# A transformer block on one core: the written-out order of all engines and the PSUM banks replaced, waits sorted, unused constants removed

## The chip, the core and the metric

One NeuronCore of a Trainium2 chip runs the whole program in one launch. Five engines have a queue of their own and run it in order: PE (matmuls), ACT (activations), DVE (elementwise work and PSUM readout), POOL (a few small operations) and SP (issues every DMA). They meet only in semaphores. The metric is the device time of one execution in microseconds. Three runs of the kernel before gave 1084.05, 1085.04 and 1085.25 us; the median is 1085.04.

## The reference: what is computed

Input `x` has 2048 rows of 1024, in bfloat16. With LN a layer norm without weights:

```
q = (LN(x) @ wq) in 32 heads of 32;  k = LN(x) @ wk;  v = LN(x) @ wv     # k, v: one head, shared
h = x + (softmax(q k^T / sqrt(32)) v, heads joined) @ wo
g = LN(h) @ w_gate;  u = LN(h) @ w_up                                   # 1024 -> 3584
out = h + (sigmoid(g) * u) @ w_down                                     # 3584 -> 1024
```

## The kernel before

**Tiles.** The rows are cut into 16 tiles of 128. Attention works on half tiles: one of 32 `hf` values takes 128 queries and 16 of the 32 heads, so 4 groups of 32 partitions by 512 columns. One *visit* (`emit_S`, L858) takes one `hf` and one of 16 blocks of 128 keys: four score matmuls that run side by side on 32 rows of the array each (row mode) fill four of six score banks of PSUM (`S_ps`), and two exponentials on ACT, 128x1024 each, write probabilities into a slot of `Pr`. There are 512 visits and 1024 exponentials. `mk_PV` multiplies probabilities by values (four matmuls side by side on 32 columns each, column mode), DVE adds the probabilities up (`make_add`, L850), `mk_SUM` sums them over the keys, and `finish` divides. `mk_OP` applies `wo` for a tile, and DVE adds `x`, takes the statistics and normalises.

**Feed-forward.** For each tile 14 groups `mk_GU` follow (7 slices of 512 columns, each a gate group *g* and an up group *u*; 8 matmuls of 512 columns): ACT takes tanh of *g* into one buffer `tnh` (L1246), DVE forms (tanh+1)*u into `act_s` (L1267), and a DMA transposes it into `hact`. Two groups `mk_D` of 28 matmuls each apply `w_down`. Gate and up weights stream from HBM through a ring and, at the end, through the free slots of `Pr` (`load_next`, 256 KB per DMA).

**Array modes.** Scores run in row mode. Between two visits a matmul of 128 columns of weights runs whole (dense) unless a column-mode group lies between the same two visits; then it is issued as four quarter matmuls (`choose_modes`, L152), so that the array changes its mode only twice a visit.

**Two working banks.** All groups but the scores (PV, SUM, OP, Q, KV, GU, D, the transposes; 472 of them) accumulate in the two banks of `F_ps`. A group is numbered when the planner begins it (`begin`, L1337), and its bank is the digit of `BANKS` under that number. The first matmul of a group waits until the group before it in the same bank has been read out by ACT or DVE.

**The order.** A planner (`Plan`) runs the program on estimated costs and gives one list of operations per engine. `reorder` (L113) then permutes each list by a string in `ORDER`: pairs of characters, of which the first says how far the next piece lies beyond the lowest operation not yet taken, and the second how many operations in a row are taken. All five engines run exactly that order. The lists hold 5757 operations on PE, 1152 on ACT, 1090 on DVE, 60 on POOL and 1017 DMAs on SP.

**The waits.** `emit` (L1518) keeps the largest value to wait for on each semaphore and issues the waits in the order in which the dependencies stand:

```
for d in o.deps + [d for d in o.order if d.eng != e]:
    ...
    if d.val > want.get(k, (0, None))[0]:
        want[k] = (d.val, s)
for k, (val, s) in want.items():
    if waited.get(k, 0) < val:
        eng.wait_ge(s, val)
```

**Constants.** `TUNE["bc"]` is 0, so `ONCHIP` is empty and `mk_BC` is never called; `pickt` (POOL, three operations) and `third` (DVE, three operations) are computed and never read.

Of the kernel before, what the change touches and what calls it, by code (L numbers as in the profile page):

```python
# [8 lines left out]
F32 = mybir.dt.float32  # L9
ACTF = mybir.ActivationFunctionType  # L10
ALU = mybir.AluOpType
# [16 lines left out]
        '0~0B32030=21020A12010~0i32030e72070iq4g20g08120105210201q392090f120102q892090f210209q3j20j01a204030252050242'  # L28
        '040252050242040252050242040252050242040252050242043272529103014202410201520501a22702014204034204033202680103'
        '013203034204033203034204033203034203560102034204024204033701a2020102420403420403320302y1f20f0h01320303225802'  # L30
        '014802abndX1l2Yc0201220203s6A142B404015203v8o202010e210202a631624282ihg2030821020o26020s26020gq832030f320301'
        '0u28020h28020362060o2202j2y4D20j0dk2010h027201a305j201020b7207c604e8u2m8w508t20t0g210208a762060202a205220201'
        '0b41125101010512010e12010V12010382320303011201a4024204021201a202a24204021201a204220202041b010311010513011201'
        '05120108120106124801010d220201110101613203010d22020722020321012401a35205030122020461220202051301622202020431'
        '0302120104622202020k12010g1201061242010102120101a203320182019101022202a2033203020122020512010528c1a202051201'
        '0512010522020542040422020j110171013203010212010612010812010512012502011201a104320301031501015132610301a23203'
        '052202230222014801010224015201320304220207220204320151015201012202a201b152c1050201220204320304220135a282c101'
        '0322020361420403220132010233030322020722020432030181083203054204034201720182c1026202044204034202510222015203'
        '110102427104015205226242810182e20102420151926101022101210101420242015182010203b20b0332030472529303b202510201'
        '01320234a27201010332030542026a0201e2010241012272439201420403420402420402513268f2e1h3033203582202010412010532'  # L40
        '03723402710111520103018208720371035101016203215201a2017203a20101040152050452025202a2010501520501c20c52050162'
        '0601820801520264c2a2e2030101625185e20552a273c3i2010263c2920291c2i201010153c2820192d101i2010164d2019101920252'
        '01610163c201810202018208620603620601820837031101320306320303420253020101420403326101610201420334927101012202'
        '01420245b2910191010242130103a202a3f2080204320304520503320302825205013203019102420171030103322154b292d1020152'
        '4172018102a273c1010152025103014202510201520502320303420405420402420402a382d208032202028102220202021201082202'
        '07220221012252017101042202042202a104320161023101032201b1010332030233030385080312010l73520283d1b2e1030528b202'
        '0103a13203034201210102a1420403420102033203033203043203034204327352a203022202024278040124020a81080d2202024103'
        '4222610101a3f14201f103b172040b12010812010d13010382080612010p124501816292010518011201011101021201410401120105'
        '12010615017232030202120105124201010312010f22020812010512010c22020722013101041301042202072201c101a101a15201a2'
        '01b1e101b202010322020241025201210101029252050222020253320303227702a1d203h10203b162c202c101c203020242011253e2'  # L50
        '01060162158101520502520501520344b2820191c101420403520113610152050152050332030532030518010e220208120101110102'
        '12010b410405a30132e101e20201620305a2052202010422114601041601410141030q2501610112c3010332910301011201a1051201'
        '0121010d120102a1031281016103430102320304320304220204320231010322020a51017352a102920203a56206020122a202060312'
        '01061201038232a1030312010512010632030342040542040332030522020542830462a802010242015801c202014404013201620241'
        '920204034204024204a1025205013203044304014204054202a1d10201629301b40405320303320304320305420403320302a482e208'
        '0222020118010655c3a205021282019103420161014104220203a2320303420202924204032202042502032102031801021201052202'
        '02734202810181016101011201052202042801a2010102a1013203042202021242316101042202011352417201110132030632030231'
        '6142030332125601320164c1a2d102a1024211010202b20b028152050132030462060342040242040542040252237501f201017903f5'
        '01j501e203i50102b2e80301k2i201l201k10101c2040102720701625185e20501018207920106016206015232780304340301320304'
        '3203236202010432a4g2e2030581b2920801a262060152010202520512620103054204034204045205024204045295g2e2o301q2l201'  # L60
        'r3030202h30202b103050d82080532030r87080I58i8v503x3020503f501j30105510155019101910203350172020683080283056103'
        '01840571030Z'),
    act=(
        '0a11010411010211010211010211010311010211010~0w12010615010113010b13010711010R11010411010511010911010t11010i11'
        '010g11010k11010711010o11010411010411010b11010711010y13010412010211010711010c12010q12010211010711010311010711'
        '010c11010811010h11010311010611010d11010b11010x11010611010311010l11010r11010q11010a11010611010i11010611010x11'
        '010z11010b12010311010h12010c11010511010511010311010611010s11010i12010j12010311010k11010512010k12010911010311'
        '010311010g'),
    dve=(
        '012251416101680108110121021301311251714161840113615101349171013201713101110101113151210121011241319201025211'  # L70
        '0131011132d16101810141015101f1610101312171115191010141013102215201410231022101032102011101011101051101110104'
        '21020151124131610103110105110111018101b1110141c17101c1910111d10151016101114101110131011101120111010311010115'
        '7361b1a1c10112014102110102110101120101210201310381011201021161310102061g01052111011101011101619101a191029101'
        '11a191b10102011201110101110111010111011501210211310101011131012151010131010101210211010113010131030131011101'
        '11011101011101021101031101190102120103110102110106710421117151410101011101124101012102022102011bd10121010721'
        '0205810411310171320111316101114101012102110121021eg1f10104130101110101a102c10231029101a131020171010232010121'
        '022102021571619181a6011101061101011141215131618101010113010311010321021101210218010411010613010a126132010102'
        '114101110111012102114101021241315c0111010b11010221110103110111010112011201110101113101010315716181a191b1d1c1'
        'e1011101032111010111010181061171310101110101110111011101011101041351416ah1g1i2010321020121012101110113514161'
        '810141310131010111011101011101210211011101021b01053101311101210271011101043111010107110111010111011101033102'  # L80
        '27a191c1b1e2d10105120101110102113121427261a20131011101210131010111310101110106146151719181a1c1b1011201011101'
        '11010211010271b10711410101021101110103110105135141620106210201110103110102124101010d'),
    pool=(
        '04d1h1g102d1c101f301h701n104k201l101le01y90101'),
    sp=(
        '01110111011101077151312161410202211152a2410191b1a1018211k121m1f101i131g2116121n1d1q2o181l1f1w1y171u1B4p1m191'
        'b1A1s141j1I1G1x1k1z1e1H1v101c1l1h1k10121a181c101a16131b181i1d141c1e10102210141612211510101110101120104511101'
        '110121011101814101410141014101012101413121010112011101110101715141910151b10161c1023101510101012101215541d1a1'
        '0181012252013371b1610101310152413171012111318142013151410153011101011101091101110131114121629401016101216251'
        '318101010212428171a16191g1f1h1b2k1j1i1l101j1l1k1a2m1o1n1q1p1r6y1A1G1z1C30181a2g1d141c1j2e1h1l1f1i1n2s3r1B1q1'  # L90
# [72 lines left out]
MARG = {"sl": 700.0, "rb": 1000.0, "rd": 1200.0, "ha": 900.0, "hT": 200.0, "ql": 1200.0, "xr": 1500.0, "o": 1400.0, "qs": 900.0, "wd": 700.0}  # L163


class Plan:
# [1429 lines left out]
```

## Time and profile before

| what | value |
|---|---|
| median of three runs | 1085.04 us (1084.05 to 1085.25) |
| profiled execution: span, from the first to the last instruction | 1083.9 us |
| profiled execution: its own time | the page gives the span alone; the median lies 1.1 us above it |
| PE | 1068.8 us busy (99%), 10588 matmuls |
| ACT | 1002.9 us busy (93%), 1008 exponentials into `Pr` of 1077 ns |
| DVE | 866.3 us busy (80%) |
| POOL | 36.1 us busy (3%) |
| DMA | 234.24 MB, 216 GB/s on average |
| mean granted TensorE clock | 0.998 |

The page gives an engine as busy from the start of an instruction to its end. Matmuls overlap: one of 512 columns is shown with 380 ns, while the next starts 216 ns after it. So 99% busy does not say that PE lost 1% only; what it loses is read from the starts of consecutive matmuls. A number in brackets in a timeline row is the time that the engine stood idle before it, and the engine whose work ended that wait.

### The profile page before, as it was taken

What the parts mean: (1) busy time and instruction counts of PE and PEld (TensorE: products, weight loads), DVE (VectorE), ACT (ScalarE), POOL (GpSimd) and SP (SyncE); (2) the same over time, 40 slices, a digit from 0 to 9 for tenths busy, and PEclk for the clock granted to TensorE, in tenths of its full rate; (3) what the DMA queues carried; (4) which work ended last, traced back from release to release, by engine and by line L of the source; (5) the groups of instructions that cost most, each with busy time, mean ns of one, the idle gap of its engine ahead of it and who ended that gap; (6) DMA issues with size and microseconds to landing.
All of it is one profiled execution on the core that took longest, in us unless ns stands there. A gap on an engine that the chain in (4) does not pass through costs nothing.

```text
span 1083.9 us, 25911 instructions
## 1 busy us (share of the span) xinstructions
PE 1068.8 (99%) x10588; PEld 432.3 (40%) x10588; DVE 866.3 (80%) x1090; ACT 1002.9 (93%) x1153; POOL 36.1 (3%) x64
## 2 busy tenths in 40 slices
PE   7999999999999999999999999999999999999998
PEld 6533465333333333333333333333333333333343
DVE  8989997887888887896888788888788878888721
ACT  5999999999999999999999999999999999999310
POOL 3300000000000000000000000000000000000000
PEclk9999999999999999999999999999999999999999
DMA  8767797799767796957968685967848796696994
GB/s 248 120 199 219 213 289 222 221 228 249 226 180 222 189 259 162 275 167 202 277 167 226 173 254 162 269 190 195 253 124 257 222 252 165 196 266 150 316 315 125
DMA packets 298935, 234.24 MB, mean 216 GB/s; under 512 B 102080, under 2 KB 285376, under 8 KB 298816
## 3 DMA queue, kind: packets, MB, share of 16 engines
q1 hardware_dynamic: 298816, 232.58, 77.2%
q8 instruction: 84, 1.38, 0.6%
q14 instruction: 35, 0.29, 0.1%
HBM read 203.55 MB, written 8.11 MB: 195 GB/s over the span
## 4 chain that ended last, share of the span: by engine, by line
PE 81%; ACT 15%; DVE 2%; issue 1%; SPq 1%; DMA 1%; DVEq 0%
PE F_ps L601 59%; ACT Pr L879 13%; PE S_ps L601 13%; PE F_ps L605 9%; ACT tnh L1246 1%; DMA ring<-in_A_x_dram 1%; SPq L453 1%; DVE acc L850 0%; DVE rb L928 0%; SPq L462 0%; ACT QTb L879 0%; ACT hnT L879 0%; ACT hact L879 0%; ACT hact L421 0%; DVE h_sb L1314 0%
## 5 line engine op out<-in xcount | busy, mean ns | idle before, releaser
L879 ACT ACTIVATE Pr<-S_ps 128x1024 bf16<-128x1024 f32 x1008 | 944.0, 1077 | 2.3 <-PE S_ps L601 2.0
L850 DVE TENSOR_TENSOR acc<-acc,Pr 128x2048 bf16<-128x2048 bf16 x429 | 522.9, 1220 | 28.7 <-ACT Pr L879 10.3
L601 PE MATMUL F_ps<-ring,hnT 128*128 128x512 bf16 x1312 | 334.5, 380 | 0.9 <-DVE h_sb L1314 0.3
L601 PE MATMUL S_ps<-QTb,kT 32*128 32x512 bf16 x2048 | 208.1, 385 | 2.1 <-ACT Pr L879 1.6
L601 PE MATMUL F_ps<-zone,hact 128*128 128x512 bf16 x732 | 202.2, 380 | 0.0
L601 PEld LDWEIGHTS F_ps<-ring,hnT 128*128 128x128 bf16 x1312 | 115.0, 97 | 155.9 <-issue 45.3
L601 PE MATMUL F_ps<-Pr,Vt 128*32 128x512 bf16 x2016 | 138.6, 382 | 2.3 <-ACT tnh L1246 1.0
L1267 DVE SCALAR_TENSOR_TENSOR act_s<-tnh,F_ps 128x512 bf16<-128x512 f32 x105 | 71.9, 685 | 82.3 <-PE F_ps L601 69.9
L601 PEld LDWEIGHTS S_ps<-QTb,kT 32*128 32x128 bf16 x2048 | 53.4, 91 | 209.4 <-ACT Pr L879 129.3
L1246 ACT ACTIVATE tnh<-F_ps 128x512 f32<-128x512 f32 x112 | 71.5, 639 | 48.0 <-PE F_ps L601 48.0
L601 PEld LDWEIGHTS F_ps<-zone,hact 128*128 128x128 bf16 x732 | 65.7, 98 | 86.8 <-issue 22.9
L605 PE MATMUL F_ps<-ring,hnT 128*32 128x512 bf16 x1104 | 76.6, 380 | 0.1
L601 PEld LDWEIGHTS F_ps<-Pr,Vt 128*32 128x32 bf16 x2016 | 47.1, 96 | 58.5 <-issue 14.6
L601 PE MATMUL F_ps<-zone 128*128 128x512 bf16 (+3 forms) x537 | 65.0, 266 | 2.4 <-DVE rstd L523 0.9
L601 PE MATMUL F_ps<-wo_sb,OT 128*128 128x512 bf16 x243 | 62.9, 380 | 0.2 <-ACT tnh L1246 0.2
L1034 DVE TENSOR_TENSOR oun<-F_ps,oun 128x512 f32<-128x512 f32 x64 | 44.0, 688 | 23.8 <-PE F_ps L601 23.4
L520 POOL TENSOR_TENSOR dsb<-zb,cst 128x1 bf16<-128x1 bf16 x18 | 17.7, 983 | 964.3 <-DVE zb L517 901.5
L605 PE MATMUL F_ps<-zone,hact 128*32 128x512 bf16 x656 | 48.1, 381 | 0.0
L601 PEld LDWEIGHTS F_ps<-zone 128*128 128x128 bf16 x537 | 34.9, 97 | 25.0 <-issue 7.9
L850 DVE TENSOR_TENSOR acc<-Pr 128x2048 bf16<-128x2048 bf16 x31 | 37.2, 1201 | 0.9 <-ACT Pr L879 0.8
L1097 DVE TENSOR_TENSOR h_sb<-F_ps,h_sb 128x512 bf16<-128x512 f32 x32 | 22.1, 691 | 19.6 <-PE F_ps L601 18.8
L605 PEld LDWEIGHTS F_ps<-ring,hnT 128*32 128x32 bf16 x1104 | 26.4, 96 | 27.4 <-issue 10.2
(94 smaller groups left out, 456.1 us busy)
## 6 DMA issues: line engine op xcount, KB each, us to landing
ring<-in_B_w_up_dram SPq DMA_DIRECT2D x312, 256.0 KB, 4.4
ring<-in_B_w_gate_dram SPq DMA_DIRECT2D x310, 256.0 KB, 4.3
rb<-r_scratch SPq DMA_DIRECT2D x120, 64.0 KB, 3.4
zone<-in_B_w_down_dram SPq DMA_DIRECT2D x14, 512.0 KB, 5.2
Pr<-in_B_w_gate_dram SPq DMA_DIRECT2D x18, 256.0 KB, 5.3
ring<-in_A_x_dram SPq DMA_DIRECT2D x16, 256.0 KB, 6.7
h_sb<-in_A_x_dram SPq DMA_DIRECT2D x16, 256.0 KB, 4.4
out_dram<-h_sb SPq DMA_DIRECT2D x32, 128.0 KB, 3.9
```

The costliest lines, as they stand in the source:

```text
L453: x_ld[t] = dma(lambda: SP.dma_start(x_sb(t), xf[t * P:(t + 1) * P, :]), f"x{t}", P * D * 2, prio=0)
L520: g = pl.op("pool", lambda: POOL.tensor_tensor(out=dsb[:, ph, tk], in0=zb[:, ph, tk], in1=half[:, 0:k], op=ALU.pow), [f, c0], prio=0, **sl ...
L601: return lambda: PE.matmul(o, lhsT=l, rhs=r, start=start, stop=stop, **kw)
L605: f.quads = [(lambda j=j: PE.matmul(o[DH * j:DH * (j + 1)], lhsT=l[:, DH * j:DH * (j + 1)], rhs=r, start=start, stop=stop, tile_position=( ...
L850: "dve", lambda lo=lo, hi=hi: DVE.tensor_tensor(out=a[:, lo:hi], in0=src[:, lo:hi], in1=slot[:, lo:hi], op=ALU.add),
L879: exps[u] = pl.op("act", lambda i=i, pb=pb: ACT.activation(out=slot[:, i * 1024:(i + 1) * 1024].rearrange("p (a b) -> p a b", a=2), in_=S_ ...
L1034: oun_ev[(hf, part)] = pl.op("dve", lambda: DVE.tensor_tensor(out=o, in0=F_ps[:, b, :], in1=o, op=ALU.add), [last, oun_ev[(hf, part - 1)]] ...
L1097: h_ev[(t, dc)] = pl.op("dve", lambda: DVE.tensor_tensor(out=h_sb[:, t % NHB, sl], in0=F_ps[:, b, :], in1=h_sb[:, t % NHB, sl], op=ALU.add ...
L1246: box["a"] = pl.op("act", lambda: ACT.activation(out=tnh[:, :], in_=F_ps[:, b, :], func=ACTF.Tanh, scale=0.5), [last, box.get("e")], prio= ...
L1267: e = pl.op("dve", lambda: DVE.scalar_tensor_tensor(out=so, in0=tnh[:, :], scalar=1.0, in1=F_ps[:, b, :], op0=ALU.add, op1=ALU.mult), [las ...
```

## The change

Three things are changed at once.

1. All five strings of `ORDER` and the 472 digits of `BANKS` are replaced. The number of operations in each list is the same, but for those that are removed; the number of pieces goes from 1842 to 1732 on PE, 221 to 133 on ACT, 690 to 693 on DVE, 23 to 20 on POOL and 835 to 677 on SP. 315 of the 472 digits of `BANKS` differ.
2. A function `clock` is added, which runs over the final lists once at build time with a table of durations and stamps an end on each operation; `emit` sorts the waits of an instruction by that end. It adds no instruction to the program.
3. `pickt`, `third`, `r_hi`, `r_3` and `mk_BC` go: three operations on POOL and three on DVE.

Since "the last" operation of the planner's list need not be the last in the new order, places that waited for one last operation now keep a list and wait for all of its members (`blk_lasts`, `q_lasts`, `d_last`, `gu_lasts`, `op_lasts`); several operations of one engine still make one wait, for the largest value. `mk_D` waits for `hact` at every matmul of both halves, not of the first alone.

The diff, cut (of the strings only the ends that the prediction speaks of):

```
     dve=(
-        '012251416101680108110121021301311251714161840113615101349171013201713101110101113151210121011241319201025211'
...
+        '110115010g11011301121110121101210010e4131611181017101210121c1610221115301410111715101411101b15101j1214131010171'
...
-        c_pk = pl.op("pool", lambda: POOL.memset(pickt[:, :, :], 1.0), [c_sel], occ=60)
...
-        c_th = pl.op("dve", lambda: DVE.tensor_reduce(
...
-        c_th = pl.op("dve", lambda: DVE.tensor_scalar(
...
+        blk_lasts = [[], [], [], []]
+        q_lasts = []
...
-                    op_last[t] = last
+                    op_last[t] = op_lasts[t]
...
-            return Group("hT", atoms, lambda: [hnorm[t], gu_last[t - 2]], after)
+            return Group("hT", atoms, lambda: [hnorm[t]] + gu_last[t - 2], after)
...
-            return [d_last[t - 2]] if t >= 2 else q_store[-NQS:] if t else extra_rel
+            return d_last[t - 2] if t >= 2 else q_store[-NQS:] if t else extra_rel
...
-                         ([hact_ev[(t, ft)]] if dq == 0 else []) + ([wd_ld[ft]] if t == 0 and dq == 0 else []))
+                         [hact_ev[(t, ft)]] + ([wd_ld[ft]] if t == 0 else []))
...
-            fb = BANKS[g]
+            fb = BANKS[g] if g < len(BANKS) else b
...
         choose_modes(lists["pe"])
+        clock(lists)
...
-                        want[k] = (d.val, s)
-                for k, (val, s) in want.items():
+                        want[k] = (d.val, s, d.end)
+                for k, (val, s, _) in sorted(want.items(), key=lambda x: x[1][2]):
                     if waited.get(k, 0) < val:
                         eng.wait_ge(s, val)
                         waited[k] = val
```

The new function, cut to its core:

```
def clock(lists):
    ...
                s = max([free[e]] + [done[id(d)] + see.get((d.eng, e), 40) for d in o.deps])
                if e == "pe":
                    m = "row" if o.kind in ("S0", "S1") else "col" if o.kind == "col" or len(o.fns) == 4 else "dense"
                    if m != mode:
                        s = max(s, free[e] + 102.0)
                        mode = m
                    free[e] = s + (7.0 if o.kind == "S0" else max(28.8 if m == "col" else 25.2, o.n / 2.4 + 2.4))
                    end = s + max(28.0, o.n / 2.4) + 170.0
                elif e == "sp":
                    ...
                    end = bus + 700.0
                else:
                    free[e] = s + o.occ
                    end = s + o.lat - SEM
                done[id(o)] = o.end = end
```

More of the change, by code (lines that the diff above doesn't have):

```diff
@@ L83 @@
     pool=(
-        '04d1h1g102d1c101f301h701n104k201l101le01y90101'),
+        '04c1e1a2d1f101f701l201m304l301n401q2010g'),
     sp=(
[L86 to L89, printed above, removed]
@@ L163 @@
 MARG = {"sl": 700.0, "rb": 1000.0, "rd": 1200.0, "ha": 900.0, "hT": 200.0, "ql": 1200.0, "xr": 1500.0, "o": 1400.0, "qs": 900.0, "wd": 700.0}
+def clock(lists):
+    see = {("act", "dve"): 32, ("act", "pe"): 53, ("act", "sp"): 25, ("dve", "dve"): 34, ("dve", "pe"): 55, ("dve", "pool"): 79,
+           ("dve", "sp"): 27, ("pe", "act"): 37, ("pe", "dve"): 37, ("pe", "sp"): 31, ("pool", "dve"): 34, ("pool", "pe"): 55,
+           ("pool", "pool"): 57, ("sp", "dve"): 24, ("sp", "pe"): 46, ("sp", "pool"): 53, ("sp", "sp"): 17}
+    at = {e: 0 for e in lists}
+    free = {e: 0.0 for e in lists}
+    done, mode, bus = {}, "dense", 0.0
+    while any(at[e] < len(lists[e]) for e in lists):
+        moved = False
+        for e in lists:
+            while at[e] < len(lists[e]):
+                o = lists[e][at[e]]
+                if any(id(d) not in done for d in o.deps + o.order):
+                    break
+                s = max([free[e]] + [done[id(d)] + see.get((d.eng, e), 40) for d in o.deps])
[7 more added lines that the diff above has]
+                elif e == "sp":
+                    k = o.key.rstrip("0123456789_")
+                    free[e] = s + o.occ
+                    bus = max(bus, s + 1720.0) + o.nbytes * (2.5 if k == "ha" and o.nbytes < 200000 else Plan.SLOW.get(k, 1.1)) / TUNE["rate"]
+                    end = bus + 700.0
+                else:
+                    free[e] = s + o.occ
+                    end = s + o.lat - SEM
+                done[id(o)] = o.end = end
+                at[e] += 1
+                moved = True
+        assert moved, "the order of the engines does not close"
 class Plan:
@@ L351, in bass_sequential_preLN__grouped_kv_mqa__glu_gated_glu__prompt_kernel @@
         r_sb = SB("r_sb", [64], F32)
-        r_hi = SB("r_hi", [64])
-        r_3 = SB("r_3", [64])
-        pickt = SB("pickt", [8, 4])
-        third = SB("third", [4], F32)
         rb = SB("rb", [512], F32)
@@ L712, in blk_done @@
             blk_left[blk] -= 1
+            blk_lasts[blk].append(last)
+            q_lasts.append(last)
             if blk_left[blk] == 0:
-                load_wd(2 * blk, last)
-                load_wd(2 * blk + 1, last)
+                load_wd(2 * blk, blk_lasts[blk])
+                load_wd(2 * blk + 1, blk_lasts[blk])
         def wd_after_q(last):
@@ L720, in wd_after_q @@
                 for i in range(8, NFT // 2):
-                    load_wd(i, last, 5)
+                    load_wd(i, q_lasts, 5)
         def mk_Qc(c, qd):
@@ L933, in after @@
                 rc = pl.op("dve", lambda: DVE.reciprocal(r_sb[:, :], F_ps[:, b, 0:64]),
[L934 to L947 removed]
+                           [last, rd_ld.get(hf - 1)], prio=0, occ=480, lat=560 + SEM)
                 pl.quiet = (pl.free["pe"], pl.free["pe"] + TUNE["quiet"])
@@ L951, in after @@
                     rb[DH * j:DH * (j + 1), :], bass.AP(r_dram.tensor, r_dram.offset + 512 * j, [[0, DH], [1, 512]])),
-                    "rb", 65536, [rd_ld[hf], ot_ev.get(hf - 2) if ONCHIP else ot_ev.get(hf - 1), ot_ev.get(0)], prio=0) for j in range(4)]
+                    "rb", 65536, [rd_ld[hf], ot_ev.get(hf - 1), ot_ev.get(0)], prio=0) for j in range(4)]
                 finish(hf)
@@ L955, in mk_SUM @@
             return Group("SUM", atoms, lambda: [add_op.get((hf, NT - 1)), c_sel], after, sum_gate)
-        ONCHIP = tuple(h for h in range(NH) if h % 2 and h not in RAW + WIDE) if TUNE["bc"] else ()
-        r_used = {}
-        bc_last = {}
-        def mk_BC(hf):
-            def pk(bb, j):
-                x = pickt[:, bb, j:j + 1]
-                return bass.AP(x.tensor, x.offset, [list(x.ap[0]), [0, DH]])
-            def atoms(b):
-                return [([mm(F_ps[DH * j:DH * (j + 1), b, bb * 64:(bb + 1) * 64], pk(bb, j), r_3[:, :],
-                             True, True, tile_position=(0, DH * j)) for j in range(4)], 64, "col", [])
-                        for bb in range(8)]
-            def after(b, last):
-                bc_last[hf] = last
-                c, hh = hf // 2, hf % 2
-                ot_ev[hf] = pl.op("dve", lambda: DVE.tensor_tensor(
-                    out=OT[:, 4 * hh:4 * hh + 4, :], in0=oun[:, hf % 2, :].rearrange("p (a b) -> p a b", a=4),
-                    in1=F_ps[:, b, :].rearrange("p (a b) -> p a b", a=4), op=ALU.mult),
-                    [last, oun_ev[(hf, len(parts_of(hf)) - 2)], op_last.get(c - 1)], prio=0, occ=600, lat=690)
-                for dc in range(2):
-                    queues["OP"].append(mk_OP(c, dc))
-                return [ot_ev[hf]]
-            return Group("SUM", atoms, lambda: [r_used[hf], oun_ev.get((hf, len(parts_of(hf)) - 2)), c_pk], after)
         def finish(hf):
@@ L1081, in bass_sequential_preLN__grouped_kv_mqa__glu_gated_glu__prompt_kernel @@
         gu_last = {}
-        d_last = {}
+        d_last = collections.defaultdict(list)
+        gu_lasts = collections.defaultdict(list)
+        op_lasts = collections.defaultdict(list)
         d_done = collections.Counter()
@@ L1245, in after_g @@
             def after_g(b, last):
+                gu_lasts[t].append(last)
                 box["a"] = pl.op("act", lambda: ACT.activation(out=tnh[:, :], in_=F_ps[:, b, :], func=ACTF.Tanh, scale=0.5),
@@ L1251, in after_u @@
             def after_u(b, last):
+                gu_lasts[t].append(last)
                 if held_w:
@@ L1286, in after_u @@
                 if i == NGR - 1:
-                    gu_last[t] = last
+                    gu_last[t] = gu_lasts[t]
                     load_hT(t + 2)
@@ L1312, in after @@
                 d_done[t] += 1
-                d_last[t] = last
+                d_last[t].append(last)
                 e = pl.op("dve", lambda: DVE.scalar_tensor_tensor(
```

167 lines of the change are left out of this document (71 added, 96 removed).

## The prediction, made before the result was known

> **What bounds the kernel now.** The page's first part, its chain and its costliest group come first.
>
> ```profile
> PE 1068.8 (99%) x10588; PEld 432.3 (40%) x10588; DVE 866.3 (80%) x1090; ACT 1002.9 (93%) x1153; POOL 36.1 (3%) x64
> ...
> PE 81%; ACT 15%; DVE 2%; issue 1%; SPq 1%; DMA 1%; DVEq 0%
> ...
> L879 ACT ACTIVATE Pr<-S_ps 128x1024 bf16<-128x1024 f32 x1008 | 944.0, 1077 | 2.3 <-PE S_ps L601 2.0
> ```
>
> PE carries the chain, ACT the rest. The windows by stage show where:
>
> ```profile
> 20.00:120.00 100.00, 98.69 (x1139) 46.49 (x1137) 92.28 (x164) 100.00 (x119) 13.62 (x26) 1.00 0.69 178
> ...
> 700.00:1000.00 300.00, 299.47 (x2910) 111.10 (x2907) 247.74 (x290) 299.99 (x343) 5.64 (x6) 1.00 0.75 208
> 1000.00:1084.00 84.00, 80.33 (x418) 34.70 (x415) 31.24 (x44) 17.68 (x24) 0.55 (x1) 1.00 0.90 251
> ```
>
> From 20 to 1010 us PE and ACT are both full; after the last exponential (about 1011.7) PE works alone for 72 us. PE does the same matmuls in any order, so the time is PE's work plus what PE loses. The timeline gives both prices: a score visit, then dense matmuls, and a long run of D.
>
> ```profile
> 607.47 0.10 PEld L601 LDWEIGHTS S_ps<-QTb,kT 32*128 32x128 bf16 x4 [0.42 <-ACT Pr L879]
> 607.48 0.39 PE L601 MATMUL S_ps<-QTb,kT 32*128 32x512 bf16 x4
> ...
> 607.80 2.12 PE L601 MATMUL F_ps<-ring,hnT 128*128 128x512 bf16 x9
> ...
> 1067.32 13.33 PE L601 MATMUL F_ps<-zone,hact 128*128 128x512 bf16 x61
> ```
>
> The run gives (13.33 - 0.38) / 60 = 0.216 us a matmul; visit to next start is 0.32 to 0.33, so a change of mode costs 0.11. Columns at that rate and 1034 changes of mode make 1053 us for PE in the old order, the 60 warm-up matmuls included. From the first transposes at 9.02 to the end of PE at 1080.5 the trace has 1071.5, for 1050 us of it: PE loses 21 us, about half of it in pieces of some 10 ns between groups. Pieces over 30 ns sum to some 12 us, 4 of them between 157 and 167, 3 before 20 us, and 0.7 only after 1010.
>
> **The new order, read from the strings.** I applied the new strings, by the rule of `reorder`, to the planner's lists, without the six removed operations. The lists are those of before: a list of last operations ends when its latest member does, so the other edits move nothing in the planner. The strings' lengths fit, every dependency closes, and no two groups overlap in a bank.
>
> *Modes.* 1034 changes become 1041: 7 x 0.11 = **+0.8 us**, all beside visits.
>
> *Banks.* What a bank needs between two groups is read here:
>
> ```profile
> 1013.72 0.40 PE L601 MATMUL F_ps<-acc,ones 128*32 128x512 bf16 x4
> 1014.05 3.41 PE L601 MATMUL F_ps<-zone,hact 128*128 128x512 bf16 x15
> 1014.17 3.39 DVE L928 RECIPROCAL rb<-F_ps 128x128 f32<-128x128 f32 x4 [0.61 <-PE F_ps L601]
> ...
> 1017.71 1.89 PE L601 MATMUL F_ps<-ring,hnT 128*128 128x512 bf16 x8 [0.25 <-DVE rb L928]
> 1019.64 0.60 ACT L1246 ACTIVATE tnh<-F_ps 128x512 f32<-128x512 f32 x1 [7.93 <-PE F_ps L601]
> ...
> 1080.69 0.69 DVE L1314 SCALAR_TENSOR_TENSOR h_sb<-F_ps,h_sb 128x512 bf16<-128x512 f32 x1 [5.35 <-PE F_ps L601]
> ```
>
> The run of 61 has its last columns in by 1080.49; DVE starts 0.20 later and takes 0.69; PE starts some 0.06 after a readout: **0.95** for a DVE readout. For tanh, 0.20 + 0.60 + 0.06 = **0.86**. After the wide sum, 1013.94 to 1017.71 = **3.77**. Where the matmuls between two groups of one bank take less, PE stands still for the difference. The old order has this 14 times, 0.48 at most; starts of consecutive matmuls show 0.30 to 0.37 where five of these sums give 0.28, so the rule holds.
>
> After the last visit the old order has two cases: the group after the wide sum (15 matmuls and a change of mode, 3.35: loses 0.42) and 0.09 after the hT transposes. The new order has, in PE's order:
>
> - last PV, then the wide SUM, same bank, nothing between: 0.95 (the old order put four D matmuls there);
> - SUM, 14 D matmuls (3.13), a GU group, same bank: 0.64;
> - a u group, two matmuls (0.43), hT, same bank: 0.52;
> - u, three matmuls (0.65), g, same bank: 0.30;
> - tile 15's u groups 460 and 462, same bank, nothing between: 0.95;
> - its g groups 461 and 463, the same: 0.86;
> - g, three matmuls (0.65), u, same bank: 0.21.
>
> That is 4.43 against 0.51: **+3.9 us**, on the path that sets the end, for nothing but PE runs there. Lower end +2.7 (the three successions with nothing between them, alone), upper end +5: the last half of D now starts 4.96 us after the u group whose transpose it needs, against 7.12, and that way took 4.05 in the trace, though other transposes landed up to 3.8 us later after issue.
>
> A rule of the Trainium skill, "Perfetto Trace Analysis", section "Matmuls", says that independent matmul groups should rotate through PSUM banks, so that a readout runs beside the next group. The new order breaks it at 460/462 and 461/463; by the rule those two alone lose their readouts, 1.8 us, which is inside the sum above.
>
> Between 45 and 980 us of PE's stream the same sum gives 5.4 against 2.8. In the first quarter PE waits for ACT anyway (64 visits are 117 us of PE, 121 of ACT), which hides 1.0 of the difference: **+1.5**, ends 0 and +2.6.
>
> *Weights.* SP's order moves 256 KB loads. From the release of their place to the first matmul that reads them, the old order leaves 6.5 us at least, the new one 5.0 to 5.9 for six loads. In the trace release to landing took 5.1 to 6.2 (middle half, tight loads): 0.2 to 0.7 each, **+1.5**, ends 0 and +5. Behind a late load stand the next visit's scores on PE.
>
> *Start.* The string of DVE moves tile 0's chain ahead of tile 1's statistics:
>
> ```profile
> 5.13 0.21 DVE L506 BATCH_NORM_AGGREGATE mv<-st 128x2 f32<-128x12 f32 x1
> 6.27 0.69 DVE L504 BATCH_NORM_STATS2 st<-ring 128x6 f32<-128x512 bf16 x1 [0.94 <-DMA ring<-in_A_x_dram]
> 6.88 0.15 DVE L511 CAST mvb<-mv 128x2 bf16<-128x2 f32 x1
> ```
>
> L511 no longer stands behind a DMA, and the first transposes come some 0.7 us earlier. But at 17.51 PE waits for the fourth piece of `wq` (0.83 us), whose load stays eleventh on SP: the gain ends there. **0**, ends -0.75 and +0.3.
>
> *Waits.* Of an instruction's waits the trace's records show the one issued first on the instruction itself, the others on a semaphore instruction ahead of it: activations that need PE and DVE carry PE, which `emit` issues first. Sorted with the latest last, PE's wait moves to the semaphore instruction, and the activation follows it: the opposite of what is meant. Such an instruction takes 17 ns on ACT, 21 on DVE, 51 on PE. At some 40 readouts that PE waits for, +0.7 to +2; if the records mislead me, as much the other way. **+0.5**.
>
> *Constants and lists.* `third` takes 0.64 us of DVE before 10 us, beside waits for `x`; `pickt` runs at 35.9, 420 and 978.7 on an idle POOL. The lists merge into one wait per engine. Nothing.
>
> **Sum:** 0.8 + 3.9 + 1.5 + 1.5 + 0 + 0.5 = +8.2. Both engines are full in the stage, and some of PE's new waits will fall where it waited for ACT; I take half of the 4.3 us there off: **+6**. 1083.9 + 6 = 1089.9, and 1.1 from span to median: **1091**.
>
> **The rivals.** (1) *Faster.* Between 157 and 167 the old order gives ACT's visits too close together and PE starves, and then runs at half clock:
>
> ```profile
> 162.00:163.00 1.00, 0.12 (x2) 0.00 (x0) 0.05 (x1) 1.00 (x3) 0.00 (x0) 1.00 0.90 265
> ...
> 164.00:165.00 1.00, 1.00 (x15) 0.11 (x4) 1.00 (x1) 0.92 (x2) 0.00 (x0) 0.50 0.96 288
> ```
>
> If the new order spreads these visits and thereby keeps the clock, 4 us come back, and with them some of the other 5 us over 30 ns in the stage. The tail's 3.9 and the modes' 0.8 are owed first, so it decides (under 1082.9) once 7 us come back; with 8: 1085 + 4.7 - 8 = 1081.7. Against it: the new order's three closest visits (3.7 us of PE for 5.4 of ACT) are nearly as close as the old ones (3.3), only 17 us earlier. (2) *No change.* The same spreading gives back 4 us and no more, the clock's share among them: 1085 + 4.7 - 4 = 1085.7. (3) *Loads late.* The six short windows find the queue full, at 0.6 us more each, and PE's new waits at 1022 to 1026 of its stream let the clock fall once more, as after the wait at 162 (mean 0.68, 0.50, 0.50 and 0.62 in the four windows from 163, so 1.7 us): 1091 + 3.6 + 1.7 = 1096. The Trainium skill, "TensorE: Matmul & The Clock Gate", section "What's actually happening", gives the same half clock after an idle window of about 3.4 us. The trace has the half clock after some 2 us of idle only.
>
> **How the numbers follow.** Forecast (1087.3 to 1094) 0.60; rival 3 0.13; rival 2 0.15; rival 1 0.12. Under 0.2% (2.2 us) this kernel can hardly be told from no change. Slower 0.73, same 0.15, faster 0.12. For 8 in 10 the range leaves out most of rival 1 and the top of rival 3: 1084 to 1097.
>
> **What would show it.** Right: in the tail two tanh or `act_s` readouts with PE idle 0.6 to 0.9 us before a GU group, PV directly before the wide sum with a wait on `oun`, and over 75 us from the last exponential to the end. Wrong: ACT's last exponential 6 us or more before 1011 us, granted clock 1.00 through 157 to 167, or a tail of 72 us.

## The result, and the profile after

The changed kernel takes 1098.3 us (1096.8 to 1099.4) against 1084.8 for the kernel before: ratio 1.0123, 95% interval 1.0109 to 1.0137. The direction was forecast; the size was not, 13.5 us where the forecast had 6.

Three lines of the page of the changed kernel, its first part, its chain and its costliest group:

```profile
PE 1056.8 (96%) x10854; PEld 433.1 (39%) x10975; DVE 866.9 (79%) x1087; ACT 1009.0 (92%) x1153; POOL 33.9 (3%) x61
...
PE 72%; ACT 12%; DVE 7%; DMA 3%; issue 3%; SPq 2%; DVEq 0%; ACTq 0%
...
L895 ACT ACTIVATE Pr<-S_ps 128x1024 bf16<-128x1024 f32 x1008 | 947.5, 1064 | 6.2 <-PE S_ps L613 5.4
```

The span is 1097.7 for 1083.9. The chain now has 9 points less of PE, and DVE, DMA and issue come in: PE waits more often. 121 matmul records are missing in this trace (10854 of 10975), so PE's busy time can't be set against that of before; the records of the weight loads and of the other engines are complete.

The windows by stage (start and end, length, then busy time and count of PE, PEld, DVE, ACT and POOL, granted clock, DMA share, GB/s), and the two single microseconds of rival 1:

```profile
20.00:120.00 100.00, 96.94 (x1086) 45.57 (x1091) 92.16 (x163) 99.16 (x117) 12.12 (x28) 1.00 0.70 188
...
700.00:1000.00 300.00, 293.15 (x3064) 111.17 (x3101) 247.36 (x287) 299.17 (x340) 4.53 (x5) 1.00 0.75 207
1000.00:1098.00 98.00, 89.11 (x513) 37.55 (x520) 38.43 (x52) 27.35 (x35) 0.55 (x1) 1.00 0.81 234
162.00:163.00 1.00, 1.00 (x22) 1.00 (x20) 1.00 (x2) 1.00 (x3) 0.00 (x0) 1.00 1.15 368
164.00:165.00 1.00, 1.00 (x18) 0.67 (x15) 0.94 (x1) 1.00 (x2) 0.00 (x0) 1.00 0.97 299
```

ACT still works through the whole stage, but it does less in 300 us (340 instructions for 343). The starvation and the half clock at 162 to 165 are gone, and the kernel is slower all the same.

Where the time goes is read from the starts of exponentials and matmuls, in us against the kernel before:

| start of | before | changed | waits unsorted (below) |
|---|---|---|---|
| first exponential | 14.85 | -0.48 | -0.87 |
| exponential 64 | 77.69 | +0.44 | +0.16 |
| exponential 192 | 201.27 | +0.11 | -0.67 |
| exponential 512 | 513.68 | +4.80 | +1.78 |
| exponential 768 | 762.77 | +7.54 | +2.55 |
| last exponential | 1010.63 | +10.15 | +4.19 |
| last matmul | 1080.27 | +14.07 | +7.59 |

Of 14.1 us, 10 arise between 200 us and the last exponential, spread over the whole stretch, and 3.9 in the tail behind it. The tail is the forecast's. The stage is nearly five times the 2.2 us that the forecast left for it.

### The profile page after: what moved, and what is told of

It reads as the page before. It is cut to its first block, busy times and chain, and to the rows that moved or that the text cites. A ratio compares the mean times of both kernels' runs of the same rounds, so it can differ in the third digit from the quotient of the medians.

```text
span 1097.7 us, 26535 instructions
## 1 busy us (share of the span) xinstructions
PE 1056.8 (96%) x10854; PEld 433.1 (39%) x10975; DVE 866.9 (79%) x1087; ACT 1009.0 (92%) x1153; POOL 33.9 (3%) x61
## 4 chain that ended last, share of the span: by engine, by line
PE 72%; ACT 12%; DVE 7%; DMA 3%; issue 3%; SPq 2%; DVEq 0%; ACTq 0%
PE F_ps L613 50%; PE S_ps L613 12%; ACT Pr L895 11%; PE F_ps L617 11%; DVE acc L866 3%; ACT tnh L1226 1%; DMA ring<-in_B_w_gate_dram 1%; SPq L465 1%; DMA r_scratch<-r_sb 1%; DMA rb<-r_scratch 1%; DVE act_s L1248 1%; DMA ring<-in_A_x_dram 0%; DVE h_sb L1075 0%; DMA zone<-ring 0%; SPq L474 0%
## 5 line engine op out<-in xcount | busy, mean ns | idle before, releaser
L613 PE MATMUL F_ps<-ring,hnT 128*128 128x512 bf16 x1190 | 298.5, 380 | 16.8 <-issue 6.4
L613 PEld LDWEIGHTS F_ps<-ring,hnT 128*128 128x128 bf16 x1254 | 107.8, 97 | 159.4 <-issue 56.4
L613 PE MATMUL F_ps<-zone,hact 128*128 128x512 bf16 x613 | 163.7, 380 | 4.5 <-issue 2.7
L613 PE MATMUL F_ps<-Pr,Vt 128*32 128x512 bf16 x2016 | 136.2, 381 | 1.3 <-DVE h_sb L1075 0.7
L617 PE MATMUL F_ps<-ring,hnT 128*32 128x512 bf16 x1336 | 88.2, 381 | 1.1 <-DVE h_sb L1295 0.7
L613 PEld LDWEIGHTS F_ps<-zone,hact 128*128 128x128 bf16 x649 | 57.7, 98 | 76.3 <-issue 18.4
L617 PE MATMUL F_ps<-zone,hact 128*32 128x512 bf16 x988 | 68.0, 381 | 0.0
L1010 DVE TENSOR_TENSOR oun<-F_ps,oun 128x512 f32<-128x512 f32 x64 | 43.9, 686 | 12.9 <-PE F_ps L613 12.6
L617 PEld LDWEIGHTS F_ps<-ring,hnT 128*32 128x32 bf16 x1336 | 31.0, 96 | 36.0 <-issue 12.1
L1295 DVE SCALAR_TENSOR_TENSOR h_sb<-F_ps,h_sb 128x512 bf16<-128x512 f32 x32 | 22.0, 688 | 23.4 <-PE F_ps L613 19.9
```

Source lines behind the costliest of these rows:

```text
L613: return lambda: PE.matmul(o, lhsT=l, rhs=r, start=start, stop=stop, **kw)
L617: f.quads = [(lambda j=j: PE.matmul(o[DH * j:DH * (j + 1)], lhsT=l[:, DH * j:DH * (j + 1)], rhs=r, start=start, stop=stop, tile_position=( ...
L1010: oun_ev[(hf, part)] = pl.op("dve", lambda: DVE.tensor_tensor(out=o, in0=F_ps[:, b, :], in1=o, op=ALU.add), [last, oun_ev[(hf, part - 1)]] ...
L1295: e = pl.op("dve", lambda: DVE.scalar_tensor_tensor(out=h_sb[:, t % NHB, sl], in0=F_ps[:, b, 0:DW], scalar=0.5, in1=h_sb[:, t % NHB, sl], ...
```

## The experiments

Two theories stood at the start. **Theory W**: the sorted waits cost most of the stage. Readouts in the two traces pointed to it: with the reading engine idle, ACT starts its readout 0.20 us after the last columns of the group before the change and 0.26 after it. For DVE it is 0.20 before the change; after it, 62 of the 124 readouts that find DVE idle start 0.07 to 0.10 later, 37 of the 45 into `act_s` among them. **Theory Q**: the order of the engines costs it, above all DVE's adds in front of readouts, which is the largest new row of the waits (engine, line and what it waited for: us, times, longest). The changed kernel, and the same adds in the kernel before:

```profile
DVE acc L866 <- ACT Pr L895: 67.1, 110, 1.3
...
DVE acc L850 <- ACT Pr L879: 11.1, 19, 1.1
```

### The waits: the order taken back, turned, and tried on the old kernel

```
e1   -for k, (val, s, _) in sorted(want.items(), key=lambda x: x[1][2]):
     +for k, (val, s, _) in want.items():
e2   +for k, (val, s, _) in sorted(want.items(), key=lambda x: -x[1][2]):
e3   the kernel before, with clock(lists) and the change's sort
e4   the kernel before, with clock(lists) and the sort of e2
```

> The changed kernel with the waits issued in the order of the dependencies, as before the change; order of engines and banks new. The changed kernel lost 10.2 us between 200 us and the last exponential and 3.9 us behind it. Theory W (sorted waits): the waits are the larger part of the 10.2, because a readout whose wait for PE lies on a semaphore instruction starts later (ACT 0.203 to 0.263 us after its group, with ACT idle, in the two traces) and stands in every loop of PE, ACT and DVE: 1089 to 1092. Theory Q (the order of the engines, above all DVE's adds that stand ahead of readouts and wait for an exponential): the waits cost 0 to 2, so 1096 to 1098.5. My forecast had +0.5 for them: 1097.8.

> The changed kernel with the waits sorted the other way, latest first. If the first wait issued is the one that stays on the instruction, and that is the better place for the latest, this is no slower than the unsorted kernel: theory W 1088 to 1092, theory Q 1095.5 to 1098.5. If the place makes the time the other way, it is slower than the changed kernel, over 1099.

> The kernel before with nothing but the sorted waits (latest last) and the function that stamps the ends. Theory W: 1091 to 1094, the greater part of the change's loss without any new order. Theory Q: 1085 to 1087. That the sorting does what it is meant to: under 1084.

> The kernel before with the waits sorted latest first. Theory W: 1082 to 1085, the order of the dependencies having most of the latest waits first already. Theory Q: 1084 to 1086. Slower than the sorted one only if the place of the latest wait works opposite to what the traces suggest.

| order of engines and banks | waits | us | ratio to before (95%) |
|---|---|---|---|
| new | sorted, latest last (the change) | 1098.3 | 1.0123 (1.0109 to 1.0137) |
| new | order of the dependencies (e1) | 1093.3 | 1.0081 (1.0066 to 1.0096) |
| new | latest first (e2) | 1092.5 | 1.0071 (1.0048 to 1.0094) |
| old | sorted, latest last (e3) | 1087.8 | 1.0029 (1.0013 to 1.0045) |
| old | order of the dependencies (before) | 1084.8 | 1 |
| old | latest first (e4) | 1082.5 | 0.9979 (0.9970 to 0.9989) |

The sort costs 0.42% (4.6 us) in the new order and 0.29% (3.1 us) in the old one; turned round it gains 0.21% (2.3 us) in the old one. What is left without the sort (e1: the new order and banks, the constants gone) costs 0.81%, 8.8 us. e2 can't be told from e1. e1 and e3 lie between what the theories expected, and neither has it all: of the whole loss the sort is a third. Of the 10.2 us of the stage the two traces give it 6.0, but the traced execution of the changed kernel is the slowest of its four (1099.4) and that of e1 the fastest (1093.0). DVE's adds are not what the sort costs: in e1 they wait just as long (the row below), in 5 us less. How much of the rest is theirs was not tried.

```profile
DVE acc L866 <- ACT Pr L895: 65.7, 107, 1.3
```

The same readout in the two timelines, the last `act_s` (start, duration, engine, line; in brackets the idle time before). The run of D matmuls starts at the moment in which the last columns of the group to be read have streamed. The changed kernel:

```profile
1082.47 12.25 PE L613 MATMUL F_ps<-zone,hact 128*128 128x512 bf16 x55
1082.77 0.69 DVE L1248 SCALAR_TENSOR_TENSOR act_s<-tnh,F_ps 128x512 bf16<-128x512 f32 x1 [2.86 <-PE F_ps L613]
```

Its waits unsorted (e1):

```profile
1075.99 12.25 PE L613 MATMUL F_ps<-zone,hact 128*128 128x512 bf16 x55
1076.19 0.69 DVE L1248 SCALAR_TENSOR_TENSOR act_s<-tnh,F_ps 128x512 bf16<-128x512 f32 x1 [2.76 <-PE F_ps L613]
```

0.30 against 0.20, on an engine that had been idle for over 2.7 us in both.

### Which engine's waits

```
-sorted(want.items(), key=lambda x: x[1][2])
+sorted(want.items(), key=lambda x: x[1][2] if e == "dve" else 0)     # e5; "pe" e6; "act" e7
```

> The changed kernel with the waits sorted on DVE alone; PE, ACT, POOL and SP issue them in the order of the dependencies. Sorted on all it takes 1098.3, on none 1093.3. With ACT and DVE idle, a readout starts 0.203 (ACT) and 0.205 to 0.218 (DVE) after its group unsorted, 0.263 and 0.272 sorted, so some 60 ns later; PE waits for 331 readouts of DVE and 110 of ACT. If the 60 ns are what costs: DVE carries most of the 5 us, 1096 to 1097.5. If it is rather PE's own waits: at most 1094.5.

> The same with the waits sorted on PE alone. In the order of the dependencies PE's wait for the free bank, mostly the latest, already stands last, behind the waits for its own data; sorting changes little there: 1093 to 1094.5. If PE's semaphore instruction (51 ns) is the price: 1095 to 1097.

> The same with the waits sorted on ACT alone: 110 tanh and 7 of the first projections start 60 ns later, and every exponential that waits for PE and DVE. ACT is full in the stage, so what it loses there delays the visits: 1093.5 to 1096. If ACT's waits are hidden: 1092.5 to 1094.

DVE alone 1096.9 (1.0109, 1.0094 to 1.0124), PE alone 1095.1 (1.0089, 1.0073 to 1.0104), ACT alone 1094.7 (1.0088, 1.0073 to 1.0103). Over e1's 1.0081 that is 3.0, 0.9 and 0.8 us, together 4.7 where all at once cost 4.6. DVE carries it, as theory W had it. PE came out 0.6 above what was expected of it, and just inside the band for the case that PE's own semaphore instruction is a price. The parts of PE and ACT are inside their intervals and are not shown one by one.

### Place or number of the semaphore instructions

The kernel before, with one more wait that is long satisfied, on every DVE operation that waits for PE; in e11 it is issued last, in e12 first:

```
 for k, (val, s) in want.items():
     ...
+if pe_due:                          # e11: here;  e12: ahead of the loop
+    eng.wait_ge(sems["pool"], 1)    # pe_due: e == "dve" and a new wait for PE is wanted
```

> The kernel before; every DVE operation that has to wait for PE waits for one more semaphore, for a value reached at the start of the kernel (POOL's first operation). The extra wait is issued last, so it lies on a semaphore instruction ahead, and the wait for PE stays on the instruction. If the place of the latest wait is what costs: no change, 1084 to 1086. If it is the number of semaphore instructions: about as slow as with the extra wait first.

> The same extra wait, issued first: it stays on the instruction, and the wait for PE goes to the semaphore instruction. The number of instructions is that of the run with the extra wait last. If the place costs some 60 ns per readout, as the sorted kernels show: DVE readouts with DVE idle start 0.27 after their group instead of 0.205, and the time is 1088 to 1091. If the place does not matter: equal to the run with the extra wait last.

Last: 1084.2, ratio 0.9997 (0.9988 to 1.0006), no change. First: 1087.0, ratio 1.0024 (1.0014 to 1.0034), slower by 2.6 us, a little under what was expected. DVE's semaphore instructions are as many in both, 738 where the kernel before has 508, so on DVE their number costs nothing that can be measured and the place costs everything. The same readout as above, in e11:

```profile
1066.80 13.33 PE L601 MATMUL F_ps<-zone,hact 128*128 128x512 bf16 x59
1067.00 0.69 DVE L1267 SCALAR_TENSOR_TENSOR act_s<-tnh,F_ps 128x512 bf16<-128x512 f32 x1 [5.36 <-PE F_ps L601]
```

and in e12:

```profile
1068.48 13.34 PE L601 MATMUL F_ps<-zone,hact 128*128 128x512 bf16 x59
1068.74 0.69 DVE L1267 SCALAR_TENSOR_TENSOR act_s<-tnh,F_ps 128x512 bf16<-128x512 f32 x1 [5.36 <-PE F_ps L601]
```

0.20 and 0.26. Over the readouts that find DVE idle (161 and 143) the median is 0.20 in e11 and 0.27 in e12: **60 to 70 ns** for a wait that lies on a semaphore instruction in front of the operation, as the 60 ns on ACT in the changed kernel. In the changed kernel some of DVE's are late by 100, as in the two rows further up. The Trainium skill, "Perfetto Trace Analysis", section "Per-engine timelines", has an explanation that fits: an operation of DVE or ACT is decoded and put into a queue, where its own wait ends, while an instruction of the sequencer alone holds the sequencer until its wait has ended, and the next one is fetched and decoded after that. The runs show the delay and its place; that it is the decoding, they don't show.

### Where the old order's gain comes from

The sort of e4 on PE alone (`-x[1][2] if e == "pe" else 0`):

> The kernel before with the waits sorted latest first on PE alone; on all engines it gave 1082.5 against 1084.9. In the order of the dependencies ACT and DVE have PE's wait first already, and PE has the wait for the free bank last, so all of the gain should be PE's: 1082 to 1083.5. If it is ACT's or DVE's: 1084.5 to 1085.5.

1082.9, ratio 0.9986 (0.9977 to 0.9995), as expected: most of e4's gain is PE's, whose wait for the free bank stands last in the order of the dependencies. PE's weight loads stand long behind "issue", what the page calls a wait for nothing that it shows. The kernel before, then e4 with two more of its rows:

```profile
PEld F_ps L601 <- issue: 106.9, 443, 1.0
PEld F_ps L601 <- DVE act_s L1267: 3.4, 15, 0.4
PEld F_ps L601 <- DVE oun L1034: 3.7, 15, 0.4
...
PEld F_ps L638 <- issue: 82.4, 362, 0.4
PEld F_ps L638 <- DVE act_s L1304: 7.6, 32, 0.4
PEld F_ps L638 <- DVE oun L1071: 7.0, 30, 0.4
```

Part of these waits now carry the name of the readout that releases the bank, since its wait is on the instruction.

### SP's order alone

The kernel before with the new string of `sp` (e9):

> The kernel before with the new order of SP's DMAs alone; PE, ACT, DVE, POOL, the banks and the waits as before. My forecast gave the loads 1.5 us (0 to 5), because six weight loads have 5.0 to 5.9 us instead of 6.5 at least; under the old order of PE the windows are other ones, so this shows whether SP's order is worth anything by itself: 1084.5 to 1087. If the loads are the hidden cause of the stage's loss: over 1088.

1097.3, ratio 1.0116 (1.0101 to 1.0132): a miss. By the letter of the expectation the loads would be the hidden cause, but the trace loses the time in other places than the changed kernel. A transposed piece of the input comes late for exponential 20 (+1.6), 3.7 us go between exponentials 192 and 256 (PE stands still there and then runs 3.4 us at a granted clock of 0.50), and 2.4 in the tail, where weights are late (e9, waits of PE):

```profile
PE F_ps L598 <- DMA Pr<-in_B_w_up_dram: 1.9, 1, 1.9
```

These are the loads of an order that PE doesn't follow here. The run shows that the strings of SP and PE belong together (12.6 us), and says nothing on what the loads cost in the changed kernel. There the waits of PE for weights are

```profile
PE F_ps L613 <- DMA ring<-in_B_w_gate_dram: 2.4, 2, 1.5
...
PE F_ps L613 <- DMA ring<-in_B_w_up_dram: 0.2, 1, 0.2
```

### The tail: two banks exchanged, then the order

e8 exchanges two digits of `BANKS`:

```
-    '...0101110101001000101')]      # 460 to 463: 1 0 1 0
+    '...0101110110001000101')]      #             1 1 0 0
```

> The changed kernel with the digits 461 and 462 of BANKS exchanged, nothing else: tile 15's u groups 460 and 462 are then in different banks, and its g groups 461 and 463. By the prediction's rule 0.95 and 0.86 go and 0.10 comes, so from the last exponential to the last matmul 73.6 becomes 71.9, and the time 1096.6. If these stalls were set by something else (the weights, the transposes): 73.6 and 1098.3.

1096.3 (1.0103, 1.0086 to 1.0119), and yet the expectation failed: from the last exponential to the last matmul the trace has 73.4 for 73.6. In the changed kernel PE stood still twice:

```profile
1061.22 1.89 PE L613 MATMUL F_ps<-ring,hnT 128*128 128x512 bf16 x8 [0.97 <-DVE act_s L1248]
...
1065.67 1.89 PE L613 MATMUL F_ps<-ring,hnT 128*128 128x512 bf16 x8 [0.84 <-ACT tnh L1226]
```

(the bracket counts from a modelled end; by starts they are 1.13 and 1.00). In e8 it stands still once, for 1.79:

```profile
1062.56 0.60 ACT L1226 ACTIVATE tnh<-F_ps 128x512 f32<-128x512 f32 x1 [9.07 <-PE F_ps L613]
1063.26 0.69 DVE L1248 SCALAR_TENSOR_TENSOR act_s<-tnh,F_ps 128x512 bf16<-128x512 f32 x1 [3.60 <-ACT tnh L1226]
...
1064.09 1.89 PE L613 MATMUL F_ps<-ring,hnT 128*128 128x512 bf16 x8 [1.63 <-DVE act_s L1248]
```

Group 462 is a u group, and its readout on DVE needs tanh of the g group 461, which comes after it. So the bank of 462 is free only after 461, tanh and `act_s`. I had taken the two pairs to lose their readouts for their banks alone. The rule of the Trainium skill on rotating banks ("Perfetto Trace Analysis", section "Matmuls") speaks of independent groups. These two are read together, and rotating their banks only moved the loss, 2.13 to 1.79 here and 0.18 a group earlier. The 1.4 us by which e8's last exponential comes earlier lies ahead of the two digits and isn't explained by them; executions of one kernel differ by as much (1096.8 to 1099.4).

e13 moves the matmuls themselves: u 460, the last eight D matmuls of 459, g 461, u 462, g 463.

```
 pe   -  ...5y504H5U304d80808b3m406k...
      +  ...5y508y5L3080808b3m406k...
 BANKS 461 to 471:  - 0 1 0 0 1 0 0 0 1 0 1    + 1 0 1 1 0 1 1 1 0 1 0
```

> The changed kernel; of PE's order, the 40 matmuls of the groups 459 to 463 alone are moved: u group 460, the 8 last D matmuls of 459, g group 461, u group 462, g group 463, and the banks follow (462 where 459 was, 464 to 471 exchanged). Exchanging two digits did nothing to the tail, because the readout of u group 462 waits for tanh of g group 461. If that is what holds PE, this order leaves at least one group between each readout and the next group of its bank, so the stalls of 1.13 and 1.00 go: from the last exponential to the last matmul 71.5 for 73.6, and 1096.2 for 1098.3. If weights or transposes hold these groups instead: 73 and 1098.

> The same order with the waits sorted latest first: the new order mended in the two places that the runs showed. Latest first alone gave 1092.5. If the two add up: 1090.4. That is still 5 us above the kernel before, and 8 above the old order with latest first, if the rest lies in PE's order in the stage (banks, loads, 1.6 us of work moved ahead of the last visit).

e13: 1096.4 (1.0113, 1.0097 to 1.0130), tail 73.1; e14: 1091.8 (1.0065, 1.0050 to 1.0080), tail 72.3. e13's time is what was expected, its tail is not, and e14 is 1.4 us above its expectation. The two stalls are gone, and one of 1.63 has come (e13):

```profile
1056.58 0.69 DVE L1259 SCALAR_TENSOR_TENSOR h_sb<-F_ps,h_sb 128x512 bf16<-128x512 f32 x1 [8.11 <-PE F_ps L577]
1057.19 0.68 DVE L1212 SCALAR_TENSOR_TENSOR act_s<-tnh,F_ps 128x512 bf16<-128x512 f32 x1
...
1058.01 1.89 PE L577 MATMUL F_ps<-Pr,hnT 128*128 128x512 bf16 x8 [1.47 <-DVE act_s L1212]
```

DVE reads D first, as its string says, and PE now finishes D later; the readout of 460, ready over two microseconds before, stands behind it. e15 exchanges those two in DVE's string as well (`...1010c310301110102` becomes `...1010d210201110102`).

> The changed kernel with the order of PE's groups 459 to 463 as in the run with the tail reordered, and one more exchange: on DVE the readout of u group 460 goes ahead of the readout of the D group 459. With PE's order alone, the stalls of 1.13 and 1.00 gave way to one of 1.63, because DVE's readout of 460 stood in its queue behind that of 459, which PE now finishes later. If the queue is the reason: the 1.63 goes too, 71.5 from the last exponential to the last matmul for 73.6 in the changed kernel, and 1096 for 1098.3. If not: 73.1.

```profile
1056.28 1.89 PE L565 MATMUL F_ps<-zone,hact 128*128 128x512 bf16 x8
1056.58 0.69 DVE L1200 SCALAR_TENSOR_TENSOR act_s<-tnh,F_ps 128x512 bf16<-128x512 f32 x1 [6.49 <-PE F_ps L565]
1058.01 1.89 PE L565 MATMUL F_ps<-Pr,hnT 128*128 128x512 bf16 x8
1058.21 0.69 DVE L1247 SCALAR_TENSOR_TENSOR h_sb<-F_ps,h_sb 128x512 bf16<-128x512 f32 x1 [0.94 <-PE F_ps L565]
```

No bracket on PE, and 71.5 us from the last exponential to the last matmul, the number expected: 2.0 us of the tail are shown to be these two pairs. The whole kernel has 1095.4 (1.0107, 1.0084 to 1.0129), whose interval alone couldn't tell it from the changed kernel; the trace does.

So the runs show 4.6 of the 13.5 us to be the sort's and 2.0 to be those two pairs. For the rest, which the new order costs, there are only readings of traces: no run put the banks, or one of the strings of PE, DVE and ACT, back alone.

## Why the prediction was wrong

**Waits, +0.5: the step that failed.** The mechanism was the one forecast, down to which wait goes where. The term was mis-sized: 4.6 us by the runs (e1). The forecast took the duration of the semaphore record (17 to 51 ns) and 40 readouts. A readout whose wait has moved is late by 60 to 100 ns. In the trace of the changed kernel PE's wait stands on the semaphore instruction at 155 of DVE's 356 readouts of `F_ps` and at 96 of ACT's 128, and at none of either in e1. The range in the text ended at +2.

**"Halved in the stage": also wrong.** Without the waits, the terms of the order add up to 0.8 + 3.9 + 1.5 + 1.5 = 7.7, and e1 lost 8.8 by the times and 7.6 to the last matmul. Had nothing been taken off, this part would have held. By the split below the reason given for halving was right, but it pays for other terms. Differences between the starts of consecutive matmuls and the usual difference for their kinds, summed from 40 us to the last visit and put down to the last dependency that ended before them (this split is worked out by me, no run shows it):

| PE stands still for | before | e1 | changed |
|---|---|---|---|
| a bank that DVE reads | 3.6 | 6.4 | 10.3 |
| a bank that ACT reads | 2.4 | 0.5 | 0.8 |
| a DMA | 0.4 | 2.2 | 3.7 |
| score banks, held by ACT | 7.5 | 5.8 | 6.0 |
| pieces under 30 ns, and unnamed | 7.9 | 9.0 | 8.9 |
| sum | 21.9 | 23.9 | 29.8 |

The order's own stalls come to +1.8 for loads, where the forecast had +1.5, and to +0.9 for banks (+2.8 where DVE reads, -1.9 where ACT reads), where it had +1.5, or 2.6 before a discount. For score banks 1.7 less is waited. But some 1.8 us of PE's work, the 0.8 of modes among it, lie ahead of the last visit that did not before. That the sort weighs on DVE's banks shows in the last column: 3.9 of its 5.9 us.

**The tail, +3.9: right, its exact size by luck: two errors cancel.** 69.65 us became 73.57. The stalls stand where they were put: 0.97 (0.95), 0.62 (0.64), 0.58 (0.52), 0.46 (0.30), 1.13 (0.95), 1.00 (0.86) and 0.35 (0.21), in brackets the forecast, 5.1 for 4.4; the sort makes most of the difference, for unsorted they are 4.7. And some 0.8 us of PE's work had moved from the tail to the stage. PV stands directly ahead of the wide sum, as forecast:

```profile
1024.19 0.40 PE L613 MATMUL F_ps<-acc,ones 128*32 128x512 bf16 x4 [0.80 <-DVE oun L1010]
```

That the two pairs lose their readouts for their banks alone, as the forecast read the rule on rotating banks, was wrong (e8, e15).

**Start, 0; modes, +0.8: right.** The first transposes come 1.1 us earlier, the first exponential 0.5, and exponential 20 is 0.1 late. The columns and modes of the new order come to 1.0 us more by my count of them. What the removed constants and merged lists are worth by themselves was not tried.

**Weight loads, +1.5: right in kind.** PE waits for weights above all twice in the stage, 1.7 and 1.0 us by starts, the first time like this:

```profile
503.39 0.81 PE L613 MATMUL F_ps<-ring,hnT 128*128 128x512 bf16 x3 [1.51 <-DMA ring<-in_B_w_gate_dram]
```

**The rivals.** Rival 1 (*faster*) had its condition met: granted clock 1.00 from 157 to 167. From exponential 64 to 192 the changed kernel gains 0.3 us (123.58 to 123.25; 122.75 in e1), not 4: what PE no longer lost there at once, it lost in small waits around. The clock's share of these 4 us, 1.7, was sized about right, but the old order keeps the full clock in some executions too. e12 has the PE order of the kernel before, stands still in the same place, and runs on at 1.00:

```profile
162.00:163.00 1.00, 0.07 (x2) 0.00 (x0) 0.06 (x1) 1.00 (x3) 0.00 (x0) 1.00 0.91 283
...
164.00:165.00 1.00, 1.00 (x19) 0.71 (x16) 0.99 (x1) 1.00 (x2) 0.00 (x0) 1.00 0.84 271
```

The same matmuls from there to the second visit after it take 3.20 us in e12 and 4.76 in the kernel before. Of the kernel before's own executions beside the experiments, the 22 with a mean granted clock of 1.000 have a median of 1083.4 us and the 34 with 0.998 one of 1084.9. Rival 3 came nearest, with 1096, but not by its mechanism: its 3.6 us for loads came on top of the forecast's 1.5, the split has 3.3 for all of them, and the clock fell nowhere.

## What to carry to other kernels

An instruction that waits for several semaphores should carry the latest wait itself; which one that is has to be looked up in the compiled program, since here the first wait issued stays on the instruction. The old order with nothing but its waits issued latest first is the fastest version of this study: 1082.5 us, 0.9979 of before (0.9970 to 0.9989). And an order is one thing over all queues: a matmul group moved on PE alone was held by DVE's queue (e13), two banks exchanged alone were held by the pair's common readout (e8), and SP's string under another PE cost 12.6 us (e9).

## What was not expected of the hardware

The wait on a separate instruction costs three times what its record shows: 60 ns for a record of 17 ns on ACT and 60 to 70 for 21 on DVE; an extra satisfied wait on DVE costs nothing (ratio 0.9997). The half clock after a starved stretch of PE lasts 3.4 us (163.4 to 166.8 in the kernel before) and is worth some 1.6 us, and the same stretch brings it in one execution and not in another (e12).
